# Converting weights inside the mixing of a spectral layer: the absolute value ahead of the relu, earlier matrices, one low part by DMA

## The chip, the cores and the metric

The kernel runs on one core of a Trainium2 chip. The metric is the time of one execution in device microseconds; a median of three executions is given, and one more execution was taken with the profiler. The engines are called PE (matmuls), DVE, ACT and POOL; SP only issues transfers, and POOL issues those transfers that add to what lies in the destination.

## The reference, cut to what matters

```python
X = np.fft.rfft(x, axis=1)                       # x: 2 x 3008 x 256
Yr = Xr @ w_r - Xi @ w_i + b_r                   # the mixing
Yi = Xr @ w_i + Xi @ w_r + b_i
Yr = np.sign(Yr) * np.maximum(np.abs(Yr) - 0.01, 0.0)
Yi = np.sign(Yi) * np.maximum(np.abs(Yi) - 0.01, 0.0)
y = np.fft.irfft(Yr + 1j * Yi, n=3008, axis=1)   # 6016 tokens of 256
h = y @ w_in1;  z = (h * sigmoid(1.702 * h)) @ w_out1     # 256 -> 2048 -> 256
h = z @ w_in2;  out = (h * sigmoid(h)) @ w_out2
```

The four matrices of the two MLP layers arrive as 64-bit floats. The kernel turns them into 32-bit floats itself, 128 x 512 numbers at a time. That work is called a conversion here, and the change is about where conversions stand.

## The kernel before, in words

There are four stages: the forward transform by matrices (until about 62 us), the mixing (62 to 147 us), the inverse transform by matrices (133 to 195 us, its PE part beginning while DVE still mixes), and the two MLP layers (the other 970 us). Up to the end of the inverse transform each engine's instructions stand in the order in which the Python code issues them. Nothing is reordered, so an instruction that waits holds up all that stands behind it on its engine.

**The mixing** is a loop of twelve turns, one for each unit (a batch, a parity, a block of 128 frequencies). In turn i the code issues, in this order:

- PE: the matmuls of unit i (`mid_mm`, L539 for units 0 and 1, L542 and L545 for the rest) into two PSUM banks. There are four banks for even and four for odd units, and the inverse transform uses the same eight.
- the sums of unit i-1 (`mid_sd`): ACT copies one bank (`us`, L551), DVE adds and subtracts (`sd`, L553 to L555). With L555 the banks are free again.
- the splits of the inputs of later units into a rounded high part and a low part (`xsplit`): ACT writes the negated value (L478), POOL adds the value by DMA (`xl`, L479), ACT casts the high part (L482).
- DVE: the folds of unit i-2 (`mid_fold`, `f`, L578; two more operations, L584 and L585, in some units).
- ACT: the relu of unit i-1 (`th`, L561), then `pump()`, then DVE's minimum (L566, `mid_th`).
- in turns 8, 10 and 11, SP: a pair of inverse matrices (`load_m`, `m<-in_mi`, L137). The fourth pair is loaded at step 0 of the inverse transform.
- at the end of turns 1, 3, 5, 7 and 9, a new conversion (`window`).

**A conversion** (`cv_bits`) begins with an absolute value on ACT (`cv_c<-raw`, L175). It reads `raw`, of which there is one buffer, and writes `cv_c`, of which there is one too. Then six closures are put on a list: five DVE operations (L180 to L184, "the bits") and one that issues POOL's adding DMA `cv_a<-cv_c` (L185) and SP's load of the next `raw` (L162, L163 or L166). `pump()` runs that list. So the next absolute value waits for two transfers: the load of `raw`, and the DMA that still reads `cv_c`.

**Placing**: a finished conversion is split into a rounded high part and a low part. `place_in` makes four sums on DVE (L213 to L216) and calls `split`. With `lo_eng="D"` ACT writes the negative (L105) and the high part (L107) and POOL adds the source by DMA (L106); with an engine given, ACT writes the high part (L109) and that engine subtracts (L110).

**The inverse transform** has sixteen steps of two banks. For each, DVE adds and subtracts (`rt`, `ac`, L406, L672 to L688), ACT copies one bank (`eo`, L668), and POOL adds results into `yt` by DMA (L722). Placings and two conversions stand among the steps.

Of the kernel before, what the change touches and what calls it, by code (L numbers as in the profile page):

```python
# [8 lines left out]

F32 = mybir.dt.float32  # L10
CFG = {'lv0': 'V', 'lv': 'V', 'dd0': 'VPVVPPPPPVVP', 'dd': 'V', 'ths': 'VVVVPV', 'thf': 'V', 'ivf': 'V', 'cva': 'P', 'pol': 'PPPP', 'pil': 'P', 'mvl': 'PVVP', 'xl': 'V', 'xse': 'V', 'gl': 'VPPPPPPP', 'tf': [6, 10, 13], 'tm': [1, 3, 5, 7, 9], 'ml': [], 'pk': 6, 'ti': [3, 7], 'pi': 4, 'pl': [1, 4, 8, 10, 13], 'kb': [0, 1, 1, 1, 1, 1, 1, 0], 'kr': [0, 1, 0, 1, 0, 1, 1, 0], 'fa': 3, 'xp': [2, 4, 4, 5], 'xq': [1, 4, 1], 'xs': 4, 'xi': [7, 7, 9, 10, 10, 11, 8], 'xsi': 9, 'xo': (0, 1, 6, 2, 3, 4, 5), 'xd': (0, 1, 4, 6), 'ca': 4, 'tl': True, 'fwd': 'all', 'rest0': 'all', 'rest1': 'all', 'last1': 'all', 'inv': 'all', 'mid': 'all', 'last0': 'all', 'thm': 'A', 'gl0': 'PVPVVVPV', 'gl2': 'PPPPPPPP', 'gl3': 'PPPPPPPV', 'xl0': 'VVVVVPV', 'xl1': 'V', 'pre': 13, 'pre2': 0, 'yd': 6, 'lvb': 6, 'mlp': 'all', 'pr': 'V', 'pf': 'V', 'eo': '0111', 'n32': 2, 'li': [8, 10, 11], 'lii': [0], 'xa': 4, 'nhb': 6, 'ddb': 6, 'mlp1': 'all', 'mlp2': 'all'}
NUM = dict(li=[5, 6, 7, 8], n32=2, pk=4, ydp=2, lii=[1, 3], xd=(), ml=[], pl=[], xo=range(7), pi=6, nhb=6, tf=[5, 9, 13], tm=[1, 3, 5, 7, 9, 11], ti=[0, 2, 4, 6, 8, 10, 12, 14, 14, 15, 15], kb=[2] * 8, kr=1, fa=3, fe=2, pm=0, nf=4, lvb=6, ddb=8, ivb=1, eob=1, fsb=6, f1=3, f2=0, fm=[7, 8, 9], fi=[1, 1, 2, 2], pre=13, pre2=1, yd=3, psh=0, ie=[12], xp=[1, 3, 4, 5], xq=[1, 2, 2], xs=5, nw=4, xi=[14, 14, 15, 15], xsi=13, rw=2, ca=4, cc=2, tb=1, tmn=1)

DEF = dict(pr="V", pf="V", lv0="V", lv="VPP", dd0="VVVVVP", dd="VPV", mpl="PV", ths="VP", thf="VVPP", fsl="VP", ivf="PPVV", cva="P", pol="P", pil="P", mvl="V", xl="PPVVPPP", xl0="PPVVPPP", xl1="PPVVPPP", xse="VP", gl="P", gl0="P", gl2="P", gl3="P", wcl="V", thc="V", thm="V")
# [42 lines left out]
def spectral_mlp_kernel(ctx, tc, xin, mfwd, minv, wc, bias, w_in1, w_out1, w_in2, w_out2, outT):  # L57
    nc = tc.nc
# [34 lines left out]
    cv_p = opened("cv", "left", 2)  # L93
# [56 lines left out]
    loaded, bits, added, fill = [], [], [], []  # L150
# [15 lines left out]
                nc.sync.dma_start(out=raw[:, :].rearrange("p (r d) -> p r d", r=2), in_=src)  # L166
            loaded.append(((kind, l, p, kept), raw))

    def cv_bits(raw, tag="a"):
        w = raw.bitcast(U32).rearrange("p (n t) -> p n t", t=2)  # L170
        hf = raw.bitcast(F32).rearrange("p (n t) -> p n t", t=2)[:, :, 1]
        c = cv_p.tile([P, 2 * CU], F32, tag="c", name="cv_c", bufs=1)
        a = cv_p.tile([P, 2 * CU], F32, tag=tag, name="cv_a", bufs=3 if tag == "a" else 1)
        cu, au = c.bitcast(U32), a.bitcast(U32)
        nc.scalar.activation(c, hf, AF.Abs, scale=2.0**-112)  # L175
        ts, stt = nc.vector.tensor_scalar, nc.vector.scalar_tensor_tensor
        band, bor, shl = ALU.bitwise_and, ALU.bitwise_or, ALU.logical_shift_left
# [57 lines left out]
    def settle(now=False):  # L235
        pump()
        ended[:] = []
        for u, (a, c) in bits:
            if not u[3]:
                spilled[u[:3]] = d = dram_p.tile([P, 2 * CU], F32, name=f"w_{u[0]}{u[1]}_{u[2]}")  # L240
                nc.sync.dma_start(out=d, in_=a)
        fresh = [(u, a) for u, (a, _) in bits if u[3]]
        done, added[:] = (added + fresh, ()) if now else (added[:], fresh)
        bits[:] = []
        return done

    def window(k, done, now=False, tag="a"):
        for u, a in done:
            if u[0] == "in":
                sums, puts = place_in(u[1], u[2], a, nc.vector if u[2] == NPR // 2 else "D", sums_tmp)  # L250
                if now:
                    for f in (puts[0], *sums, puts[1]):
                        f()
                else:
                    fill.extend(sums + puts)
            else:
                place_out(u[1], u[2], a, nc.gpsimd if u[2] == NPR - 2 else "D")
        for _ in range(min(k, len(loaded))):
            u, raw = loaded.pop(0)
            bits.append((u, cv_bits(raw, tag)))  # L260

    def tick(k=1):
        window(k, settle(True))
# [18 lines left out]
    raws, lvs, xs = {}, {}, {}  # L282
# [307 lines left out]
    hold = []  # L590
    for i in range(len(mids)):
        ps = mid_mm(i)
        sd = mid_sd(*post) if post is not None else None
        xsplit(i + 3, 1)
        xsplit(i + 2, 0)
        if thr is not None:
            mid_fold(*thr)
        if sd is not None:
            thr = mid_relu(*sd)
            pump()  # L600
            thr = mid_th(*thr)
# [323 lines left out]
    puts = []  # L925
# [11 lines left out]
    done = []  # L937
    added.extend(hold)
    for at, (l, i, p) in enumerate(seq):
# [8 lines left out]
        k = rate(at)  # L948
# [182 lines left out]
```

## Time and profile before

| | |
|---|---|
| median of three runs | 1166.54 us (1165.54 to 1167.99) |
| the profiled execution's own time | 1166.52 us |
| its span, first to last instruction | 1164.7 us |
| PE busy | 1146.9 us (98%) |
| DVE, ACT, POOL busy | 629.7, 774.4, 477.9 us |
| mean granted clock of PE | 0.995 |

The execution's time is 1.8 us more than its span. Over the whole span PE is idle for 17.8 us. What a change to the first 195 us can win is some of that idle time, and time in which PE runs at a lower clock. In the rows below, a time in square brackets is how long the engine sat idle before that instruction, and the arrow names what ended the wait.

### The profile page before, as it was taken

Reading aid. Unit: us, or ns where it says so; the run is one execution under the profiler, and the core shown is the slowest. Engines: PE = TensorE matmul, PEld = TensorE weight load, DVE = VectorE, ACT = ScalarE, POOL = GpSimd, SP = SyncE. Lnnn points to the kernel's source line nnn. Section 1 sums busy time; section 2 is a strip of 40 time slices with the busy share of each in tenths; the row PEclk is TensorE's granted clock in tenths of the full one; section 3 lists DMA queues with packets and bytes.
Section 4 is the critical chain, followed back from the end, with each engine's and each line's share of the span. In section 5 each row is a group of like instructions: output and inputs, shape, how many; then the busy total and the mean of one; then the engine's idle time right before and its main releaser. Section 6 shows DMA issues by size and latency. Waiting matters only on the chain.

```text
span 1164.7 us, 14637 instructions
## 1 busy us (share of the span) xinstructions
PE 1146.9 (98%) x5094; PEld 949.7 (82%) x5094; DVE 629.7 (54%) x1013; ACT 774.4 (66%) x1444; POOL 477.9 (41%) x412
## 2 busy tenths in 40 slices
PE   8999899999999999999999999999999999999998
PEld 6768786887888888888889878888888888888897
DVE  7777798766365474575563553442533523523522
ACT  2576446877677667676677786665766765766755
POOL 1243134454444443444436655333433333433333
PEclk9999899999999999999999999999999999999999
DMA  8777666451121121211220100000000000000000
GB/s 295 179 142 149 149 149 119 109 113 33 49 72 37 36 73 37 60 49 37 72 55 19 55 19 19 1 37 1 1 37 1 30 7 1 37 1 1 37 1 32
DMA packets 39564, 68.49 MB, mean 59 GB/s; under 512 B 3649, under 2 KB 15809, under 8 KB 39490
## 3 DMA queue, kind: packets, MB, share of 16 engines
q1 hardware_dynamic: 26162, 45.51, 11.9%
q0 software_dynamic: 13328, 22.05, 11.2%
q8 instruction: 40, 0.66, 0.2%
q14 instruction: 34, 0.28, 0.1%
HBM read 35.15 MB, written 10.35 MB: 39 GB/s over the span
## 4 chain that ended last, share of the span: by engine, by line
PE 81%; issue 7%; ACT 3%; DVE 3%; DMA 3%; POOL 2%; SPq 0%; POOLq 0%; DVEq 0%; ACTq 0%
PE o L808 40%; PE x L836 35%; PE psf L376 4%; PE psm L539 1%; ACT yt L839 1%; DMA cv_a<-cv_c 1%; DMA wo<-cv_a 1%; POOL xl L479 1%; ACT g L841 1%; DMA raw<-in_x 1%; DVE yt L858 0%; DMA xl<-xt 0%; POOL yt L722 0%; ACT x L747 0%; DVE yt L887 0%
## 5 line engine op out<-in xcount | busy, mean ns | idle before, releaser
L846 POOL TENSOR_TENSOR g<-yt,g 128x512 fp32r<-128x512 f32 (+1 forms) x282 | 362.7, 1298 | 495.8 <-PE x L836 332.0
L808 PE MATMUL o<-g,wo 128*128 128x512 f32 (+1 forms) x2304 | 560.1, 385 | 0.5 <-DMA wo<-cv_a 0.5
L836 PE MATMUL x<-x,wi 128*128 128x512 f32 (+1 forms) x2016 | 498.8, 386 | 3.5 <-ACT yt L877 1.9
L808 PEld LDWEIGHTS o<-g,wo 128*128 128x128 f32 x2304 | 432.4, 188 | 81.5 <-DMA wo<-cv_a 1.0
L836 PEld LDWEIGHTS x<-x,wi 128*128 128x128 f32 x2016 | 377.0, 188 | 80.4 <-ACT yt L877 4.9
L839 ACT ACTIVATE yt<-yt 128x512 f32<-128x512 f32 (+1 forms) x288 | 179.1, 622 | 253.6 <-DVE yt L887 204.8
L841 ACT CAST g<-yt 128x512 fp32r<-128x512 f32 (+1 forms) x384 | 235.1, 612 | 12.2
L887 DVE TENSOR_TENSOR yt<-yt,x 128x512 f32<-128x512 f32 (+1 forms) x96 | 64.7, 674 | 214.3 <-PE x L836 213.7
L858 DVE TENSOR_TENSOR yt<-yt,x 128x512 f32<-128x512 f32 (+1 forms) x96 | 64.8, 675 | 167.1 <-ACT yt L855 165.2
L846 DVE TENSOR_TENSOR g<-yt,g 128x512 fp32r<-128x512 f32 (+1 forms) x102 | 70.1, 687 | 73.2 <-ACT g L841 73.2
L185 POOL DMA_DIRECT2D cv_a<-cv_c x32 | 28.1, 877 | 98.4 <-DVE cv_c L184 92.0
L891 DVE TENSOR_TENSOR yt<-yt,x 128x512 f32<-128x512 f32 (+1 forms) x96 | 64.8, 674 | 0.4 <-issue 0.3
L754 DVE TENSOR_TENSOR x<-yt,x 128x512 fp32r<-128x512 f32 (+1 forms) x44 | 46.2, 1051 | 29.6 <-ACT x L747 29.6
L875 ACT COPY yt<-x 128x512 f32<-128x512 f32 (+1 forms) x96 | 54.7, 570 | 2.9 <-PE x L836 2.9
L839 ACT ACTIVATE yt<-x 128x512 f32<-128x512 f32 (+1 forms) x96 | 56.1, 584 | 0.0
L877 ACT COPY yt<-x 128x512 f32<-128x512 f32 (+1 forms) x96 | 55.7, 580 | 0.1
L376 PE MATMUL psf<-m,xf 128*128 128x190 f32 (+3 forms) x224 | 53.2, 399 | 2.4 <-POOL xf L327 2.4
L376 PE MATMUL psi<-m,f 128*128 128x188 f32 (+3 forms) x224 | 49.0, 373 | 6.2 <-DVE sd L555 2.9
L855 ACT COPY yt<-x 128x512 f32<-128x512 f32 (+1 forms) x96 | 54.7, 570 | 0.0
L376 PEld LDWEIGHTS psf<-m,xf 128*128 128x128 f32 x224 | 39.3, 193 | 16.1 <-POOL xf L327 3.0
L376 PEld LDWEIGHTS psi<-m,f 128*128 128x128 f32 x224 | 39.7, 199 | 13.8 <-DVE sd L555 3.2
L175 ACT ACTIVATE cv_c<-raw 128x512 f32<-128x512 f32 x32 | 21.5, 673 | 19.0 <-DMA cv_a<-cv_c 8.7
(118 smaller groups left out, 817.5 us busy)
## 6 DMA issues: line engine op xcount, KB each, us to landing
raw<-in_wi SPq DMA_DIRECT2D x32, 256.0 KB, 3.7
cv_a<-cv_c POOLq DMA_DIRECT2D x32, 256.0 KB, 5.1
raw<-in_wo SPq DMA_DIRECT2D x16, 512.0 KB, 3.9
xl<-xt POOLq DMA_DIRECT2D x20, 256.0 KB, 4.3
out_t<-yt SPq DMA_DIRECT2D x20, 256.0 KB, 2.0
raw<-in_x SPq DMA_DIRECT2D x9, 512.0 KB, 6.0
w_in<-cv_a SPq DMA_DIRECT2D x8, 256.0 KB, 2.0
w_out<-cv_a SPq DMA_DIRECT2D x8, 256.0 KB, 2.0
```

What stands on the lines that cost most here:

```text
L376: nc.tensor.matmul(ps, hi[:, c : c + P], m[:, k, :w], start=i == 0, stop=i == last)
L808: nc.tensor.matmul(acc[h, mm], st, mv, start=first and k == 0, stop=last and k == 2)
L836: nc.tensor.matmul(ps, st, mv, start=first and m == 0, stop=m == 2, skip_group_check=True)
L839: nc.scalar.activation(g, g if src is None else src, func)
L841: nc.scalar.copy(gh, g)
L846: eng.tensor_sub(gl, g, r32(gh))
L855: nc.scalar.copy(y1, X)
L858: nc.vector.tensor_add(y1, y1, Y)
L875: nc.scalar.copy(y2, Z)
L877: nc.scalar.copy(y3, X)
L887: nc.vector.tensor_add(y2, y2, X)
L891: nc.vector.tensor_add(y3, y3, Z)
```

## The change

Four things change. In turns 1, 3, 5, 7 and 9 the block that starts a conversion stands ahead of the folds and the relu and no longer at the end of the turn; `pump()` still stands behind the relu, so the bits now follow in the same turn. The pairs of inverse matrices are loaded in turns 3, 5 and 7. The fifth w_in unit (p = 4) of the first layer gets its low part by DMA like the others. The buffer tag of the last conversion is now found from a number; the tags come out the same.

```diff
-'li': [8, 10, 11]        (in the long CFG line)
+'li': [3, 5, 7]
-                sums, puts = place_in(u[1], u[2], a, nc.vector if u[2] == NPR // 2 else "D", sums_tmp)
+                sums, puts = place_in(u[1], u[2], a, "D", sums_tmp)
...
         xsplit(i + 3, 1)
         xsplit(i + 2, 0)
+        if i in N('tm'):
+            ready = settle(True)
+            window(0, [r for r in ready if r[0][2] < NPR // 2 and r[0][0] == "in"])
+            hold.extend(r for r in ready if r[0][2] >= NPR // 2 or r[0][0] == "out")
+            window(1, (), n=N('tm').index(i))
         if thr is not None:
             mid_fold(*thr)
         if sd is not None:
             thr = mid_relu(*sd)
-            pump()
+        pump()
+        if sd is not None:
             thr = mid_th(*thr)
         if i in N('li'):
             load_m()
         post = (i, ps)
-        if i in N('tm'):
-            ready = settle(True)
-            window(0, [r for r in ready if r[0][2] < NPR // 2 and r[0][0] == "in"])
-            hold.extend(r for r in ready if r[0][2] >= NPR // 2 or r[0][0] == "out")
-            window(1, (), tag="ld" if i == N('tm')[-1] else "a")
```

ACT in turns 9 and 10, with the last conversion of the mixing (before with -, now with +; the numbers of raw only count buffers):

```order
 L482 CAST xh<-xt_318 128x512
 L482 CAST xh<-xt_319 128x512
+L175 ACTIVATE cv_c<-raw_1127 128x512
 L561 ACTIVATE th<-sd,neglam 128x512 x2
-L175 ACTIVATE cv_c<-raw_1173 128x512
 L551 COPY us<-psm 128x512
 L561 ACTIVATE th<-sd,neglam 128x512 x2
```

The absolute value has moved ahead of the two halves of the relu of unit 8; the same holds in turns 1, 3, 5 and 7.

DVE before, from the folds of unit 8 in turn 10 to the sums of unit 10 in turn 11:

```order
L578 TENSOR_TENSOR f_1262<-th 128x512
L578 TENSOR_TENSOR f_1264<-th 128x512
L180 TENSOR_SCALAR cv_c<-cv_c 128x512
L181 TENSOR_SCALAR cv_c<-cv_c 128x512
L182 SCALAR_TENSOR_TENSOR cv_a<-raw_1173,cv_c 128x512
L183 TENSOR_SCALAR cv_c<-cv_a 128x512
L184 SCALAR_TENSOR_TENSOR cv_c<-raw_1173,cv_c 128x512
L566 SCALAR_TENSOR_TENSOR th<-sd,th 128x512 x2
L553 TENSOR_TENSOR sd<-us,psm 128x512
L554 TENSOR_TENSOR sd<-us,psm 128x256
L555 TENSOR_TENSOR sd<-psm,us 128x256
```

DVE now, from the last conversion's bits in turn 9 to the minimum of unit 9 in turn 10, ahead of the sums of unit 10:

```order
L180 TENSOR_SCALAR cv_c<-cv_c 128x512
L181 TENSOR_SCALAR cv_c<-cv_c 128x512
L182 SCALAR_TENSOR_TENSOR cv_a<-raw_1127,cv_c 128x512
L183 TENSOR_SCALAR cv_c<-cv_a 128x512
L184 SCALAR_TENSOR_TENSOR cv_c<-raw_1127,cv_c 128x512
L566 SCALAR_TENSOR_TENSOR th<-sd,th 128x512 x2
L553 TENSOR_TENSOR sd<-us,psm 128x512
L554 TENSOR_TENSOR sd<-us,psm 128x256
L555 TENSOR_TENSOR sd<-psm,us 128x256
L578 TENSOR_TENSOR f_1276<-th 128x512
L578 TENSOR_TENSOR f_1278<-th 128x512
L566 SCALAR_TENSOR_TENSOR th<-sd,th 128x512 x2
```

The same five operations now stand one whole turn earlier: between them and the sums of unit 10 lie the sums of unit 9, the folds of unit 8 and two minimums, where one minimum lay before.

SP before, from the load of turn 5 on:

```order
L166 DMA raw_1058<-in_wo 128x2x256
L166 DMA raw_1173<-in_wo 128x2x256
L137 DMA m<-in_mi 128x768 x2
L166 DMA raw_1275<-in_wo 128x2x256
L137 DMA m<-in_mi 128x760 x2
L137 DMA m<-in_mi 128x752 x2
L137 DMA m<-in_mi 128x1128 x2
```

SP now, the same loads:

```order
L137 DMA m<-in_mi 128x768 x2
L166 DMA raw_1006<-in_wo 128x2x256
L137 DMA m<-in_mi 128x760 x2
L166 DMA raw_1127<-in_wo 128x2x256
L137 DMA m<-in_mi 128x752 x2
L166 DMA raw_1239<-in_wo 128x2x256
L137 DMA m<-in_mi 128x1128 x2
```

Three pairs now stand ahead of the raw loads of turns 5, 7 and 9, and the fourth, at step 0 of the inverse transform, directly behind the load of turn 9.

## Rows read from the trace of the kernel before

**Rows 1.** Waits of PE, 130 to 200 us: engine, line, what ended it

```profile
PE psi L376 <- DVE sd L555: 2.9, 1, 2.9
PE psi L376 <- DVE rt L406: 2.0, 2, 1.3
PE x L836 <- DVE yt L887: 0.8, 1, 0.8
PE psi L376 <- DVE rt L688: 0.8, 1, 0.8
PE psi L376 <- DMA m<-in_mi: 0.5, 1, 0.5
PE x L836 <- ACT eo L668: 0.2, 1, 0.2
```

**Rows 2.** Timeline of PE, mixing and start of the inverse: start, length, instruction

```profile
81.79 0.39 PE L542 MATMUL psm<-wh,xh 128*128 128x512 f32 x1
...
87.47 0.39 PE L542 MATMUL psm<-wh,xh 128*128 128x512 f32 x1
...
132.91 4.06 PE L376 MATMUL psi<-m,f 128*128 128x192 f32 x24
139.91 2.93 PE L376 MATMUL psi<-m,f 128*128 128x192 f32 x8 [2.94 <-DVE sd L555]
```

**Rows 3.** Stretches: length, busy PE PEld DVE ACT POOL, clock, DMA share, GB/s

```profile
140.00:146.00 6.00, 5.54 (x17) 5.04 (x18) 5.93 (x11) 2.84 (x5) 0.00 (x0) 0.50 1.00 298
147.00:160.00 13.00, 13.00 (x83) 13.00 (x82) 12.04 (x26) 4.01 (x7) 1.75 (x3) 1.00 0.19 76
160.00:190.00 30.00, 26.98 (x117) 19.65 (x116) 27.86 (x53) 18.88 (x35) 20.06 (x21) 1.00 1.11 193
```

**Rows 4.** Timeline of DVE, 132 to 156 us

```profile
132.13 0.69 DVE L553 TENSOR_TENSOR sd<-us,psm 128x512 f32<-128x512 f32 x1 [4.05 <-ACT us L551]
...
134.60 0.42 DVE L180 TENSOR_SCALAR cv_c<-cv_c 128x512 f32<-128x512 f32 x1
...
137.31 1.29 DVE L566 SCALAR_TENSOR_TENSOR th<-sd,th 128x512 f32<-128x512 f32 x2
138.51 0.68 DVE L553 TENSOR_TENSOR sd<-us,psm 128x512 f32<-128x512 f32 x1
...
142.18 0.68 DVE L553 TENSOR_TENSOR sd<-us,psm 128x512 f32<-128x512 f32 x1
...
148.63 0.55 DVE L676 TENSOR_TENSOR rt<-psi,eo 128x380 f32<-128x380 f32 x1
...
154.44 0.55 DVE L110 TENSOR_TENSOR wi<-cv_a,wi 128x384 fp32r<-128x384 f32 x1
...
155.51 0.54 DVE L687 TENSOR_TENSOR ac<-rt,psi 128x377 f32<-128x377 f32 x1
```

**Rows 5.** Timeline of ACT, 116 to 150 us

```profile
116.76 0.67 ACT L175 ACTIVATE cv_c<-raw 128x512 f32<-128x512 f32 x1 [2.58 <-DMA cv_a<-cv_c]
...
130.96 0.66 ACT L175 ACTIVATE cv_c<-raw 128x512 f32<-128x512 f32 x1 [4.52 <-DMA cv_a<-cv_c]
131.53 0.57 ACT L551 COPY us<-psm 128x512 f32<-128x512 f32 x1
...
149.87 0.48 ACT L668 COPY eo<-psi 128x384 f32<-128x384 f32 x1 [5.22 <-DVE rt L406]
```

**Rows 6.** Waits of DVE, 60 to 150 us

```profile
DVE sd L553 <- ACT us L551: 11.9, 4, 4.0
```

**Rows 7.** Timeline of POOL, end of the mixing

```profile
137.69 0.86 POOL L185 DMA_DIRECT2D cv_a<-cv_c  x1 [13.32 <-DVE cv_c L184]
```

**Rows 8.** DMA issues, 109 to 119 us: transfer, count, KB, median us to landing

```profile
cv_a<-cv_c POOLq DMA_DIRECT2D x1, 256.0 KB, 5.5
```

**Rows 9.** DMA issues, 121 to 133 us, two matrices and a raw load beside it

```profile
cv_a<-cv_c POOLq DMA_DIRECT2D x1, 256.0 KB, 7.4
```

**Rows 10.** The buffer cv_a, 60 to 210 us: landing, shortest, median, longest

```profile
DMA to landing us min/median/max: 3.2/5.6/10.0
```

More of the change, by code (lines that the diff above doesn't have):

```diff
@@ L10 @@
 F32 = mybir.dt.float32
-CFG = {'lv0': 'V', 'lv': 'V', 'dd0': 'VPVVPPPPPVVP', 'dd': 'V', 'ths': 'VVVVPV', 'thf': 'V', 'ivf': 'V', 'cva': 'P', 'pol': 'PPPP', 'pil': 'P', 'mvl': 'PVVP', 'xl': 'V', 'xse': 'V', 'gl': 'VPPPPPPP', 'tf': [6, 10, 13], 'tm': [1, 3, 5, 7, 9], 'ml': [], 'pk': 6, 'ti': [3, 7], 'pi': 4, 'pl': [1, 4, 8, 10, 13], 'kb': [0, 1, 1, 1, 1, 1, 1, 0], 'kr': [0, 1, 0, 1, 0, 1, 1, 0], 'fa': 3, 'xp': [2, 4, 4, 5], 'xq': [1, 4, 1], 'xs': 4, 'xi': [7, 7, 9, 10, 10, 11, 8], 'xsi': 9, 'xo': (0, 1, 6, 2, 3, 4, 5), 'xd': (0, 1, 4, 6), 'ca': 4, 'tl': True, 'fwd': 'all', 'rest0': 'all', 'rest1': 'all', 'last1': 'all', 'inv': 'all', 'mid': 'all', 'last0': 'all', 'thm': 'A', 'gl0': 'PVPVVVPV', 'gl2': 'PPPPPPPP', 'gl3': 'PPPPPPPV', 'xl0': 'VVVVVPV', 'xl1': 'V', 'pre': 13, 'pre2': 0, 'yd': 6, 'lvb': 6, 'mlp': 'all', 'pr': 'V', 'pf': 'V', 'eo': '0111', 'n32': 2, 'li': [8, 10, 11], 'lii': [0], 'xa': 4, 'nhb': 6, 'ddb': 6, 'mlp1': 'all', 'mlp2': 'all'}
+CFG = {'lv0': 'V', 'lv': 'V', 'dd0': 'VPVVPPPPPVVP', 'dd': 'V', 'ths': 'VVVVPV', 'thf': 'V', 'ivf': 'V', 'cva': 'P', 'pol': 'PPPP', 'pil': 'P', 'mvl': 'PVVP', 'xl': 'V', 'xse': 'V', 'gl': 'VPPPPPPP', 'tf': [6, 10, 13], 'tm': [1, 3, 5, 7, 9], 'ml': [], 'pk': 6, 'ti': [3, 7], 'pi': 4, 'pl': [1, 4, 8, 10, 13], 'kb': [0, 1, 1, 1, 1, 1, 1, 0], 'kr': [0, 1, 0, 1, 0, 1, 1, 0], 'fa': 3, 'xp': [2, 4, 4, 5], 'xq': [1, 4, 1], 'xs': 4, 'xi': [7, 7, 9, 10, 10, 11, 8], 'xsi': 9, 'xo': (0, 1, 6, 2, 3, 4, 5), 'xd': (0, 1, 4, 6), 'ca': 4, 'tl': True, 'fwd': 'all', 'rest0': 'all', 'rest1': 'all', 'last1': 'all', 'inv': 'all', 'mid': 'all', 'last0': 'all', 'thm': 'A', 'gl0': 'PVPVVVPV', 'gl2': 'PPPPPPPP', 'gl3': 'PPPPPPPV', 'xl0': 'VVVVVPV', 'xl1': 'V', 'pre': 13, 'pre2': 0, 'yd': 6, 'lvb': 6, 'mlp': 'all', 'pr': 'V', 'pf': 'V', 'eo': '0111', 'n32': 2, 'li': [3, 5, 7], 'lii': [0], 'xa': 4, 'nhb': 6, 'ddb': 6, 'mlp1': 'all', 'mlp2': 'all'}
 NUM = dict(li=[5, 6, 7, 8], n32=2, pk=4, ydp=2, lii=[1, 3], xd=(), ml=[], pl=[], xo=range(7), pi=6, nhb=6, tf=[5, 9, 13], tm=[1, 3, 5, 7, 9, 11], ti=[0, 2, 4, 6, 8, 10, 12, 14, 14, 15, 15], kb=[2] * 8, kr=1, fa=3, fe=2, pm=0, nf=4, lvb=6, ddb=8, ivb=1, eob=1, fsb=6, f1=3, f2=0, fm=[7, 8, 9], fi=[1, 1, 2, 2], pre=13, pre2=1, yd=3, psh=0, ie=[12], xp=[1, 3, 4, 5], xq=[1, 2, 2], xs=5, nw=4, xi=[14, 14, 15, 15], xsi=13, rw=2, ca=4, cc=2, tb=1, tmn=1)
@@ L167, in cv_load, with cv_bits @@
             loaded.append(((kind, l, p, kept), raw))
-    def cv_bits(raw, tag="a"):
+    def cv_bits(raw, n):
         w = raw.bitcast(U32).rearrange("p (n t) -> p n t", t=2)
@@ L172, in cv_bits @@
         c = cv_p.tile([P, 2 * CU], F32, tag="c", name="cv_c", bufs=1)
-        a = cv_p.tile([P, 2 * CU], F32, tag=tag, name="cv_a", bufs=3 if tag == "a" else 1)
+        a = cv_p.tile([P, 2 * CU], F32, tag="ld" if n == 4 else "a", name="cv_a", bufs=1 if n == 4 else 3)
         cu, au = c.bitcast(U32), a.bitcast(U32)
@@ L245, in settle, with window @@
         return done
-    def window(k, done, now=False, tag="a"):
+    def window(k, done, now=False, n=0):
         for u, a in done:
             if u[0] == "in":
-                sums, puts = place_in(u[1], u[2], a, nc.vector if u[2] == NPR // 2 else "D", sums_tmp)
+                sums, puts = place_in(u[1], u[2], a, "D", sums_tmp)
                 if now:
@@ L259, in window @@
             u, raw = loaded.pop(0)
-            bits.append((u, cv_bits(raw, tag)))
+            bits.append((u, cv_bits(raw, n)))
     def tick(k=1):
```

## The prediction

> **What bounds the kernel now.** I read the waits of PE first, since PE is busy for 98% of the span and only its gaps can be won. Between 130 and 200 us they come to 7.2 us: 2.9 us at DVE's L555, 0.5 us at an inverse matrix, and 2.0, 0.8, 0.8 and 0.2 us at operations of the inverse transform's end work [rows 1]. Next I read PE's timeline for the place of the long one. It lies inside the second step of the inverse transform: 24 matmuls run from 132.91, then PE stands for 2.94 us until 139.91 [rows 2]. The stretches then show what followed: from 140 to 146 us the granted clock is 0.50, which is 1.2 GHz, the lower of the two levels, and from 147 us on it is 1.00 again [rows 3].
>
> Then I followed the wait back. PE needs banks that DVE frees with the sums of unit 10. These begin at 138.51, though the matmuls of unit 10 were over when those of unit 11 began, 5.68 us (one unit of 25 matmuls, as from 81.79 to 87.47) before 132.91 [rows 2, 4], at about 127. DVE is some 11 us behind PE. It got there by four waits for ACT's copy, 11.9 us in all [rows 6]. The last of them, 4.05 us, ends at 132.13 [rows 4], and ACT's copy began only at 131.53, directly behind an absolute value that had itself waited 4.52 us for the DMA of the conversion before [rows 5]. So the path of the mixing is no engine's work; it is a ring: absolute value, bits, POOL's adding DMA, its landing, next absolute value. In turns 7 to 9 it took 130.96 - 116.76 = 14.2 us for two units [rows 5], and PE needs 2 x 5.68 = 11.4.
>
> **The change, part by part.**
>
> *The ring.* Before, the absolute value stood at the end of a turn and its bits came after the next unit's copy, sums and folds. Now they follow at once. What is left of the ring is ACT's 0.6 us [rows 5], from the first bit operation to the issue of the DMA 137.69 - 134.60 = 3.1 us [rows 4, 7], and the landing L: 3.7 + L. It keeps up with PE as long as L is under 11.4 - 3.7 = 7.7 us. The trace has 5.5 us for a conversion's DMA with no matrices beside it [rows 8] and 7.4 us for one with a pair of matrices and a raw load beside it [rows 9]; the longest of the whole stretch is 10.0 [rows 10]. Now each conversion of turns 3, 5 and 7 has a pair beside it, so I take the 7.4, from the same company, and keep 5.5 and 10.0 as bounds.
>
> *What queues behind the absolute value.* Where it must wait, the relu of the unit before, the next copy and the splits wait behind it on ACT, and on DVE the bits, then the minimum, then the next unit's sums. That is the same company as before, but one turn earlier against PE. DVE's own work fits: from 132.13 to 138.51 lie the sums, folds, bits and minimum of one turn, 6.4 us; the bits are 2.7 of it (134.60 to 137.31) [rows 4], so a turn without them is 3.7, and two turns take 2 x 3.7 + 2.7 = 10.1 of PE's 11.4 us. The work now moved into turn 1 is hidden by DVE's wait for PE there; without that cover it would put DVE back by the 2.7 us once, which the 1.3 us of slack in each pair of turns gives back.
>
> *The end of the mixing.* With no lag left, the sums of unit 11 begin when its matmuls end, at 132.9 instead of 142.18. Up to the first end work of the inverse transform DVE then needs what it needed before, 148.63 - 142.18 = 6.45 us [rows 4], so that work begins at 139.35 and not at 148.63: 9.3 us earlier. PE's 2.94 us go, because unit 10 is freed within 2 us of the 127 at which its matmuls end. So does the stretch at the lower clock, as its cause is gone: 5.54 us of PE work at half speed [rows 3], 2.8 us lost.
>
> *The matrices.* They now land some 30 us ahead of their use, so the 0.5 us goes [rows 1]. It would not go by the ring alone: the loads stood behind a raw load that waits for the bits. What they cost is their share of the DMA engines in turns 3 to 7, and that is in L. SP passes three pairs ahead of raw loads; each pair has two turns until the next raw load, so the queue is not what makes those wait.
>
> The Trainium skill, in "DMA: Bandwidth & Descriptors" (section "Issuing engines are not separate DMA queues"), says that transfers issued by SP and by POOL run on the same 16 DMA engines and interleave. The step from 5.5 to 7.4 us agrees [rows 8, 9]. This is the rule that speaks against the change: SP's matrices lengthen the landing that the ring consists of, and the second case below hangs on it.
>
> *The low part by DMA.* DVE loses two subtractions, 154.44 to 155.51, 1.1 us [rows 4], in a stretch in which it is busy for 12.04 of 13 us [rows 3]. ACT gets two more operations and POOL two more issues in the same place. ACT stood idle for 5.22 us just before [rows 5], and POOL was busy for 1.75 of the 13 us [rows 3]; the weights are first read in the MLP. I cost it at nothing. Without that cover it is about 1 us on ACT, and not below nothing.
>
> *The inverse transform.* DVE is busy for 27.86 of 30 us there and PE waits for it in four groups, 2.0 + 0.8 + 0.8 + 0.2 = 3.8 us [rows 1, 3]. DVE comes 9.3 + 1.1 = 10.4 us earlier. PE without any of its waits comes 2.9 + 0.5 + 2.8 + 3.8 = 10.0 us earlier. The smaller of the two decides, 10.0, with the two so close that what is late next is DVE again: any new wait of DVE beyond 0.4 us costs PE the same. For such waits (the bounds are 0, and 1.5 us if several come) I take 0.7. From 195 us on PE is the bound and nothing there is changed, so what is won stays.
>
> The sum: 10.0 - 0.7 = 9.3 us. The profiled execution took 1166.52 us, the median of the runs is 1166.54, so no correction is needed: 1157.2 us.
>
> **The rivals.**
>
> *The landing grows to about 10 us.* For it: the longest in the trace, the DMA share of 1.11 at 160 to 190 us [rows 3, 10], and turn 3 has a placing's two DMAs beside its pair. Against it: 7.4 in the nearest case [rows 9]. By the durations above the first relevant DMA is issued in turn 3 at about 88.4 us (unit 2 over at 81.79 [rows 2]; DVE's sums and folds, 3.7 - 1.2 = 2.5 us without the minimum; a placing's four sums, an estimated 1 us; then the 3.1). The absolute value of turn 9 then stands at 88.4 + L + 2 x (3.7 + L) = 95.8 + 3L, and the end work of the inverse begins 0.6 + 2.7 + 1.2 (the minimum, 137.31 to 138.51 [rows 4]) + 2 x 3.7 + 6.45 = 18.3 us later, at 114.1 + 3L. With L = 10 that is 144.1, which is 4.5 us earlier than before; with 1.1 for the subtractions DVE wins 5.6: 1160.9 us. From L = 8.4 on this case takes over from the forecast.
>
> *The same formula, on the other side.* For L = 11.9 DVE wins nothing (114.1 + 35.7 = 149.8 against 148.63 + 1.1); above that the change is slower, as the ring now holds the relu back three times while the matrices pass. At L = 13 it begins at 153.1, DVE is 3.4 us late and PE's hole is that much longer: 1166.5 + 3.4 = 1169.9 us. Against it: no landing over 10.0 in the trace.
>
> *The inverse stage is paced by its DMAs.* At 160 to 190 us the DMA share is 1.11 [rows 3], and these adding transfers, not DVE, may set when its buffers come free. Then the waits of 3.8 us stay and the new ones come near their size: 10.0 - 3.8 - 3.0 = 3.2 us won, 1163.3. Against it: nearly all waits of PE there name DVE or ACT [rows 1].
>
> *It does not do what it says:* the landing of raw, not of `cv_a`, ends the wait anew, and the ring is as long as before: 1166.5.
>
> **How the numbers follow.** The forecast (landing up to 8.4 us) has a chance of 0.66, and by itself a range of 1155.8 to 1159.0. The landing near 10 has 0.15, the DMA-paced inverse stage 0.08, no effect 0.05, the slower case 0.06. A measurement of this kernel can tell 0.2%, 2.3 us, from no change. Faster by that: 0.66 + 0.15 + 0.07 = 0.88; within it 0.06; slower 0.06. For 8 in 10 the range takes the forecast's own, half a microsecond of scatter below it, and the case of 10 us above it with a little of what lies beyond: 1155.3 to 1162.0.
>
> **What would show it.** Right: PE's timeline has no gap of more than 1 us between 127 and 150 us, and the granted clock is 1.00 there; DVE's waits for ACT's copy in the mixing fall from 11.9 us to under 3; ACT's absolute values in the mixing wait for under 2 us in all; the end work of the inverse begins at 139 to 140 us; DVE runs no L110 there; the last wait of PE before the MLP ends near 185 us and not at 195. Wrong: absolute values of turns 5, 7 and 9 that wait for `cv_a` by 2 us or more, each longer than the one before (landing near 10); PE waits in the inverse stage that stay at 3.8 us or grow, and name DMAs (paced by DMAs); a stretch at the lower clock anywhere from 100 to 190 us.

## The result and the profile after

The changed kernel takes 1155.70 us (median of four runs, 1155.53 to 1157.88) against 1167.26 us for the kernel before beside it (four runs, 1165.54 to 1168.42): a ratio of 0.9906 [0.9888, 0.9925], some 11 us faster. The profiled execution took 1155.86 us with a span of 1154.1, which is 10.6 us shorter than the span before. The forecast was 1157.2, within 1155.3 to 1162.0, so the measured time lies near the lower end of the range.

The waits of PE after, 130 to 200 us, stand against the six of [rows 1]:

```profile
PE x L837 <- DVE yt L888: 0.9, 1, 0.9
PE psi L376 <- DVE rt L689: 0.6, 1, 0.6
PE x L837 <- ACT eo L669: 0.2, 1, 0.2
```

The wait for L555, the matrix and the two waits for L406 are gone. What stays is the end of the inverse transform, where PE has nothing else left to run. PE's timeline after has no stop where [rows 2] have one of 2.94 us:

```profile
131.31 6.01 PE L376 MATMUL psi<-m,f 128*128 128x192 f32 x36
...
138.43 0.48 PE L376 MATMUL psi<-m,fd 128*128 128x188 f32 x2
...
151.00 18.89 PE L376 MATMUL psi<-m,f 128*128 128x190 f32 x94
170.46 4.06 PE L376 MATMUL psi<-m,f 128*128 128x376 f32 x12 [0.57 <-DVE rt L689]
...
184.05 2.35 PE L837 MATMUL x<-x,wi 128*128 128x512 f32 x9 [0.85 <-DVE yt L888]
```

The stretches after (columns as in [rows 3]) have the clock at 1.00, the upper level, where it was 0.50 from 140 to 146 us:

```profile
130.00:140.00 10.00, 10.00 (x61) 9.77 (x60) 7.67 (x14) 2.60 (x5) 0.00 (x0) 1.00 0.01 2
140.00:150.00 10.00, 10.00 (x64) 10.00 (x63) 9.66 (x21) 4.21 (x8) 5.13 (x5) 1.00 0.46 75
```

ACT's absolute values and POOL's adding DMAs after answer to [rows 5, 7]; this is the ring itself:

```profile
81.95 0.66 ACT L175 ACTIVATE cv_c<-raw 128x512 f32<-128x512 f32 x1
94.55 0.66 ACT L175 ACTIVATE cv_c<-raw 128x512 f32<-128x512 f32 x1 [1.14 <-DMA raw<-in_wi]
106.08 0.68 ACT L175 ACTIVATE cv_c<-raw 128x512 f32<-128x512 f32 x1 [1.31 <-DMA cv_a<-cv_c]
117.70 0.67 ACT L175 ACTIVATE cv_c<-raw 128x512 f32<-128x512 f32 x1 [2.84 <-DMA cv_a<-cv_c]
```

```profile
86.95 0.86 POOL L185 DMA_DIRECT2D cv_a<-cv_c  x1 [0.61 <-DVE cv_c L184]
98.34 0.86 POOL L185 DMA_DIRECT2D cv_a<-cv_c  x1 [4.81 <-DVE cv_c L184]
109.89 0.86 POOL L185 DMA_DIRECT2D cv_a<-cv_c  x1 [5.00 <-DVE cv_c L184]
```

From 94.55 to 98.34 is 3.8 us of work (3.7 was forecast), and from that issue to the next absolute value 7.7 us; the next turn has 3.8 and 7.8. A turn of the ring, from one absolute value to the next, is 11.5 and 11.6 us where the one in [rows 5] took 14.2. The absolute values of turns 7 and 9 still wait for `cv_a`, the second longer than the first; that of turn 5 waits for the load of `raw`. But at the end of the mixing DVE is not late any more, as its timeline against [rows 4] shows:

```profile
131.58 0.69 DVE L553 TENSOR_TENSOR sd<-us,psm 128x512 f32<-128x512 f32 x1 [1.83 <-PE psm L542]
...
138.03 0.55 DVE L677 TENSOR_TENSOR rt<-psi,eo 128x380 f32<-128x380 f32 x1
...
154.10 0.55 DVE L688 TENSOR_TENSOR ac<-rt,psi 128x377 f32<-128x377 f32 x1 [0.31 <-DMA yt<-ac]
```

The sums of unit 11 now wait for PE. They began at 142.18 and begin at 131.58, and the end work of the inverse follows after the same 6.45 us, at 138.03. L110 does not run there any more. No wait of DVE from 60 to 150 us names ACT's copy any more, where [rows 6] have 11.9 us. Two waits of the bits for their absolute value are there:

```profile
DVE cv_c L180 <- ACT cv_c L175: 2.2, 2, 1.3
```

One more wait names the absolute value, the one of 3.49 us ahead of the first sums. The name misleads: the sums do not read `cv_c`, and the kernel before waits as long at the same place, for PE's matmuls of unit 0. So it is no waiting for ACT. Before, then after:

```profile
69.24 0.69 DVE L553 TENSOR_TENSOR sd<-us,psm 128x512 f32<-128x512 f32 x1 [3.48 <-PE psm L539]
```

```profile
67.64 0.69 DVE L553 TENSOR_TENSOR sd<-us,psm 128x512 f32<-128x512 f32 x1 [3.49 <-ACT cv_c L175]
```

**How much of the 10.6 us is the change.** Not all. The mixing's matmuls ended at 132.91 and now end at 131.31, and the first conversions already stand 1.6 us earlier. The difference arises in the first 62 us, where the change moves nothing: in the execution before, the granted clock was lower from 10 to 15 us. One row of each, before and then after, with the columns of [rows 3]:

```profile
10.00:15.00 5.00, 5.00 (x11) 2.50 (x11) 4.09 (x8) 0.68 (x4) 1.91 (x6) 0.70 1.06 408
```

```profile
10.00:15.00 5.00, 4.55 (x14) 2.77 (x15) 3.67 (x8) 1.20 (x6) 1.08 (x5) 1.00 1.03 394
```

This differs from one execution to the next and not with the order: of the experiments below, the third has the old order and a clock of 1.00 there (mixing over at 131.27), the fourth the new order and 0.66 (132.97). Against an execution with the same clock at the start the spans differ by 1163.5 - 1154.1 = 9.4 us (third against after, which differ in the order and the matrices alone) and 1164.7 - 1156.4 = 8.3 us (before against fourth, without the low part). From the first matmul of the inverse to PE's last wait before the MLP it is 195.25 - 132.91 = 62.34 us before and 184.05 - 131.31 = 52.74 after: 9.6 us won in the stage that the change acts on. Of the 10.6 us, 1.6 are the start, 9.6 this stage, and about 0.6 are given back in the MLP; 0.4 of these are PE's waits there, which grew from 2.7 to 3.1 us.

### The profile page after: what moved, and what is told of

Read it like the earlier page. It is cut to its first block, busy times and chain, and to the rows that moved or that the text cites. A ratio compares the mean times of both kernels' runs of the same rounds, so it can differ in the third digit from the quotient of the medians.

```text
span 1154.1 us, 14647 instructions
## 1 busy us (share of the span) xinstructions
PE 1141.7 (99%) x5094; PEld 946.7 (82%) x5094; DVE 628.4 (54%) x1011; ACT 775.9 (67%) x1446; POOL 478.4 (41%) x414
## 3 DMA queue, kind: packets, MB, share of 16 engines
q0 software_dynamic: 13616, 22.51, 11.5%
## 4 chain that ended last, share of the span: by engine, by line
PE 92%; ACT 2%; DVE 2%; issue 2%; DMA 1%; POOL 1%; SPq 0%; POOLq 0%; DVEq 0%
PE o L809 42%; PE x L837 37%; PE psm L542 5%; PE psf L376 4%; PE psi L376 3%; PE psm L539 1%; ACT yt L840 1%; DMA raw<-in_x 1%; ACT x L748 0%; DVE yt L859 0%; DMA yt<-ac 0%; ACT yt L856 0%; DMA wo<-cv_a 0%; DVE x L755 0%; ACT g L842 0%
## 5 line engine op out<-in xcount | busy, mean ns | idle before, releaser
L376 PE MATMUL psi<-m,f 128*128 128x188 f32 (+3 forms) x224 | 45.3, 358 | 0.6 <-DVE rt L689 0.6
L748 ACT CAST x<-tmp 128x512 fp32r<-128x512 f32 (+1 forms) x36 | 22.1, 613 | 17.6 <-DVE tmp L757 15.7
```

The lines of the kernel that those rows point to most:

```text
L376: nc.tensor.matmul(ps, hi[:, c : c + P], m[:, k, :w], start=i == 0, stop=i == last)
```

## The experiments

The theory was the ring: the mixing is paced by absolute value, bits, DMA and landing, and the new order shortens it. The rivals were that the matrices or the low part bring the gain, and that the ring's landing L grows until it costs what the order wins. Each kernel was compared with the kernel before on the same chip.

**1. Only the order.** The block ahead of the folds and the bits in the same turn; `li` stays [8, 10, 11], and the low part stays on DVE.

> Only the new place of the conversions in the mixing; matrices in turns 8, 10 and 11 and the subtracting low part as before. Ring theory (the late conversions made DVE late, and that made PE's gap and the lower clock): the 2.94 us gap and the stretch at 1.2 GHz go, absolute values of turns 5, 7, 9 wait under 1 us in all since no matrices run beside the first two, DVE reaches the end work of the inverse at about 138 to 139 us; but the matrices of turns 10 and 11 stand behind turn 9's raw load only, so they still come early enough (issue near 122 to 129, landing 5 to 9 us); DVE keeps the 1.1 us of subtractions, so PE's waits in the inverse grow by about 1: 8 to 9 us faster than before, 1158. Rival (the early matrices carry the gain): the gap stays at 2 to 3 us and the time is within 2 us of before.

Measured: 1156.79 us, ratio 0.9921 [0.9906, 0.9935]. The order alone brings 9.5 us against 1166.29 for the kernel before. Its absolute values hardly wait:

```profile
104.72 0.67 ACT L175 ACTIVATE cv_c<-raw 128x512 f32<-128x512 f32 x1
115.12 0.67 ACT L175 ACTIVATE cv_c<-raw 128x512 f32<-128x512 f32 x1 [0.22 <-DMA cv_a<-cv_c]
```

The landings of turns 5 and 7 are 4.9 and 5.4 us there and the ring 10.3 to 10.4 us, yet the end work begins at 138.07, as in the changed kernel: PE is the bound. The wait of 0.5 us for a matrix went too, against my claim that it needs the earlier loads. I expected PE's waits in the inverse stage to grow by about 1 us against the changed kernel; they are 1.9 us against 1.6.

**2. Only the matrices, at turns 3, 5 and 7 in the old order.**

```
-'li': [8, 10, 11]
+'li': [3, 5, 7]
```

> Only the earlier matrices (turns 3, 5, 7). Ring theory: the gap at the second step of the inverse and the lower clock stay, since the ring is as long as before; the 0.5 us at a matrix goes; the conversions' DMAs of turns 4, 6 and 8 now run beside matrices and land in 7 to 8 us in place of 5.3 and 5.5, so DVE is later by 2 to 4 us at the sums of unit 10 and the gap grows to 4 to 7 us: 1 to 5 us slower than before. Rival (the early matrices carry the gain): 5 us faster or more.

Measured: 1166.59 us, ratio 0.9995 [0.9982, 1.0008]: no difference, where I expected a loss. I had counted the pairs that are added beside conversions but not the pair of turn 8 that leaves. The absolute value of turn 9, which waited 4.52 us in [rows 5], waits 1.95; that of turn 7 waits 4.16 us and not 2.58. PE's stop is shorter and the waits in the inverse are longer:

```profile
PE psi L376 <- DVE rt L406: 3.4, 3, 2.1
PE psi L376 <- DVE sd L555: 2.3, 1, 2.3
```

**3. Only the low part by DMA.**

```
-place_in(u[1], u[2], a, nc.vector if u[2] == NPR // 2 else "D", sums_tmp)
+place_in(u[1], u[2], a, "D", sums_tmp)
```

> Only the low part by DMA. DVE is the bound of the inverse stage: its end comes 1.1 us earlier, the gap and the lower clock stay: PE's waits there fall from 3.8 to about 2.7, 0.5 to 1.1 us faster, which is too small for the times to tell but is seen in the trace. Rival (what stands on DVE in the inverse stage is what counts most): 3 us or more.

Measured: 1166.42 us, ratio 0.9998 [0.9989, 1.0006]. Alone, the low part brings nothing that can be measured: PE still stops for 3.33 us at L555 and waits 2.5 us for L406. I expected its waits in the inverse stage to fall from 3.8 to about 2.7 us; they are 4.4. The lower clock behind the stop lasts about half as long here as before: 0.57 from 138 to 142 us and 1.00 from 142 to 146, where the kernel before has 0.66 and 0.50.

**4. Order and matrices, without the low part.**

> The whole change but for the low part, which DVE subtracts as before. Ring theory: like the changed kernel up to the first step of the inverse (no gap, clock 1.00, end work from about 138 us), then PE's waits in the inverse stage larger by about 1.1 us (2.7 in place of 1.6): 1156.5 to 1157. Rival (the subtraction on DVE decides): 1159 or more.

Measured: 1157.3 us, ratio 0.9917 [0.9903, 0.9932], the same as the order alone. The matrices lengthen the ring (absolute values wait 1.42 and 2.54 us for `cv_a`, landings of turns 5 and 7 of 7.9 and 7.4 us), but the PE waits from 130 to 200 us are those of the first experiment, 0.8, 0.8 and 0.2. A pair issued beside the transfer is not all there is to it: in the first experiment the matrices of turn 8 are issued 0.2 and 1.8 us behind the transfer of turn 7, and it still lands in 5.4 us.

What the low part does is seen at two places. The wait for L689 is 0.82 us here and in the first experiment, 0.57 in the changed kernel. And the 94 matmuls ahead of it take 18.89 us in the changed kernel, but 19.24 us here and 19.23 in the first experiment:

```profile
151.04 19.23 PE L376 MATMUL psi<-m,f 128*128 128x190 f32 x94
```

From the first matmul of the inverse to PE's last wait before the MLP it is 53.3 us in both, against 52.74. So the low part is worth 0.6 us on PE, where I expected 1.1 us of waits, and the order 9.0 of the 9.6 us.

**5. The changed kernel with the bits in the next turn again.** The absolute value stays ahead of the relu.

```
-        pump()
+        if i not in N('tm'):
+            pump()
```

> The changed kernel, but the bits of turns 1, 3, 5, 7 and 9 run in the next turn, as before the change; only the absolute value stays ahead of the relu. Ring theory: the ring is then longer than before the change, not shorter: absolute value, two relus, minimum, the next unit's sums and folds, bits, DMA, landing, that is about 0.6 + 1.3 + 1.2 + 1.3 + 1.2 (or 2.7) + 3.1 + 6 to 8 = 15 to 18 us for two turns against 11.4 that PE needs. The gap is back with 3 to 8 us, the clock falls again: 1166 to 1171, no gain or slower. Rival (it is the absolute value's place ahead of the relu that brings the gain): 1155 to 1158, no gap.

Measured: 1172.17 us, ratio 1.0043 [1.0028, 1.0058]: slower than before, and just above the 1166 to 1171 that I expected. The place of the absolute value is worth nothing without the bits behind it. The ring is longer than ever, and what it holds back on ACT now stops PE inside the mixing. ACT, then PE:

```profile
106.09 0.66 ACT L175 ACTIVATE cv_c<-raw 128x512 f32<-128x512 f32 x1 [6.68 <-DMA raw<-in_wi]
122.95 0.66 ACT L175 ACTIVATE cv_c<-raw 128x512 f32<-128x512 f32 x1 [8.64 <-DMA cv_a<-cv_c]
```

```profile
126.91 0.50 PE L542 MATMUL psm<-wh,xh 128*128 128x512 f32 x1 [4.53 <-ACT xh L482]
```

The turn of the ring is 122.95 - 106.09 = 16.9 us. The split `xh` of the next unit stands behind the absolute value on ACT, and PE waits for it. The other half, the bits in the same turn with the absolute value at its old place, was not run; so it is shown that the bits must follow, and not that the absolute value had to move.

**6. The kernel before with a second buffer for `cv_c`.** Conversions of turns 5 and 9 use another buffer, so from turn 5 on no absolute value waits for the landing before it; order, matrices and low part are as before.

```
-c = cv_p.tile([P, 2 * CU], F32, tag="c", name="cv_c", bufs=1)
+c = cv_p.tile([P, 2 * CU], F32, tag="tmp" if alt else "c", name="cv_c", bufs=1)
```

> The kernel before; only the conversions of turns 5 and 9 write their absolute value into another buffer (the one for sums, idle there), so that no absolute value from turn 5 on waits for the DMA that reads the buffer of the one before. Order, matrices and low part as before. Ring theory: the waits for cv_a, 2.6 and 4.5 us in turns 7 and 9, go; the ring then runs through the load of raw, 5.1 + 2.7 + 0.3 + 4.5 = 12.6 us for two turns in place of 13.7 to 14.2, so DVE is 3 to 5 us less late at the sums of unit 10: the gap shrinks to 1 us or less or goes, the clock may stay at 1.00: 3 to 6 us faster than before. Rival (DVE is late by its own work, not by the ring): gap and time as before.

Measured: 1162.98 us, ratio 0.9955 [0.9937, 0.9972]: 4.1 us faster. The ring is real, since opening it at another link helps too. The absolute values of turns 7 and 9, which waited 2.58 and 4.52 us for `cv_a`, now wait for `raw`, whose load is issued behind the bits:

```profile
117.46 0.68 ACT L175 ACTIVATE cv_c<-raw 128x512 f32<-128x512 f32 x1 [0.77 <-DMA raw<-in_wo]
128.24 0.67 ACT L175 ACTIVATE cv_c<-raw 128x512 f32<-128x512 f32 x1 [1.10 <-DMA raw<-in_wo]
```

So there are two rings, one through `cv_c` and one through `raw`, and both hold the bits. The second was there already in the kernel before; its absolute values of turns 3 and 5 wait for `raw`, the later one longer:

```profile
103.07 0.66 ACT L175 ACTIVATE cv_c<-raw 128x512 f32<-128x512 f32 x1 [4.30 <-DMA raw<-in_wi]
```

Moving the bits forward shortens both, which a buffer does not. PE's stops at 137 and 141 us are 0.67 and 1.88 us here, and the granted clock stays at 1.00 behind them.

**7. More bytes.** The changed kernel, with half again as many bytes beside each of the three pairs of matrices on SP's queue, into columns that nothing reads.

```
+            if nb * w < 1000:
+                o = cs * MW // 2 + nb * w
+                nc.sync.dma_start(out=m[:, o : o + 384], in_=minv[t // 2, q, cs][:, :384])
```

> The changed kernel, with half as many bytes again beside each of the three pairs of matrices, loaded into columns that nothing reads. Landing theory (the conversions' DMA shares the engines with them, and the mixing is late by three times what it grows): landings of the conversions' DMAs rise from 7.7 to about 9 us, the absolute values of turns 5, 7 and 9 wait for 2.5, 3.5 and 6 us in place of 1.1, 1.3 and 2.8; DVE's sums of unit 11 begin about 1 to 2 us after PE's matmuls end; 0 to 2 us slower than the changed kernel. Rival (the queue of SP does not touch POOL's DMAs): landings and waits as in the changed kernel.

Measured: 1155.85 us, ratio 0.9904 [0.9889, 0.9919]. I expected the landing to grow and it did not. The issues from 97 to 108 us, in the changed kernel and here:

```profile
xl<-xt POOLq DMA_DIRECT2D x4, 256.0 KB, 8.2
m<-in_mi SPq DMA_DIRECT2D x2, 380.0 KB, 8.0
...
cv_a<-cv_c POOLq DMA_DIRECT2D x1, 256.0 KB, 7.7
```

```profile
xl<-xt POOLq DMA_DIRECT2D x4, 256.0 KB, 9.2
m<-in_mi SPq DMA_DIRECT2D x2, 380.0 KB, 9.0
...
m<-in_mi SPq DMA_DIRECT2D x2, 192.0 KB, 10.1
cv_a<-cv_c POOLq DMA_DIRECT2D x1, 256.0 KB, 7.4
```

The matrices take a microsecond longer; `cv_a` does not. The time is what the rival gives, but its reason (SP's queue does not touch POOL's transfers) does not hold: the splits `xl`, which POOL issues behind `cv_a`, take a microsecond longer too. In the changed kernel SP's last matrix of this stretch lands at 107.05 us and `cv_a`, issued at 98.34, at 106.06. So SP's queue is busy for that whole landing already, and bytes behind it come too late to matter; the later `xl` outlast it, the last of them until 111.50, and meet the added bytes. That is how I read the rows; it was not tested further. The landing of turn 9, which gets no added bytes of its own, takes 8.5 us and not 7.9.

The Trainium skill, "DMA: Bandwidth & Descriptors" (section "Queues, rings and completion order"), says that a DMA engine takes a packet from each queue in turn. These rows agree with it (7.4 us for `cv_a` and 9.2 for `xl`); what each engine did packet by packet was not looked at.

**8. Is DVE the pace of the inverse stage?** The changed kernel with the final subtractions of the inverse transform on POOL; the final additions stay on DVE.

```
-'ivf': 'V'
+'ivf': 'VVVP'
```

> A try for a faster version: the changed kernel with one of the two kinds of final subtractions in the inverse transform (about 0.9 us each for three batches) on POOL and not on DVE. If DVE is still what PE waits for there, PE's 1.6 us of waits between 165 and 185 us go: about 1 to 1.5 us faster than the changed kernel, 1154.5. Rival (POOL's operation takes over 1.1 us and holds DVE at the shared buffers, or delays POOL's DMAs): as the changed kernel or 1 us slower.

Measured: 1161.4 us, ratio 0.9949 [0.9933, 0.9966], 5.6 us above the seventh kernel, which ran beside it. The rival was right, and by more than I put. POOL, DVE and PE of this kernel:

```profile
146.69 2.85 POOL L719 TENSOR_TENSOR yt<-rt 128x376 f32<-128x376 f32 x2 [2.42 <-DVE rt L689]
```

```profile
158.75 0.55 DVE L688 TENSOR_TENSOR ac<-rt,psi 128x377 f32<-128x377 f32 x1 [3.91 <-DMA yt<-ac]
```

```profile
159.99 11.76 PE L376 MATMUL psi<-m,f 128*128 128x376 f32 x48 [2.18 <-issue]
```

POOL's 2.85 us stand ahead of its adding DMAs, which were issued at 146.59 in the changed kernel and now at 149.50; 0.6 us of that is a later start of the inverse transform. DVE must have `ac` back from them, and waits 3.91 us where it waited 0.31. So the rival that the inverse stage is paced by its DMAs lies near: in the changed kernel DVE waits for them for only 0.31 us, and issued later they hold it for 3.91.

**9 and 10. A longer landing on POOL's own queue.** The changed kernel, with one or three copies of 256 KB to spare memory issued ahead of the adding DMA in turns 3, 5 and 7.

```
+    def copies(c):
+        for _ in range(1):          # 3 in the tenth
+            d = dram_p.tile([P, 2 * CU], F32, name=f"spare{len(spares)}")
+            spares.append(d)
+            nc.gpsimd.dma_start(out=d, in_=c)
-lambda: (nc.gpsimd.dma_start(out=a, in_=c, accum_op=ALU.add), ...
+lambda: (copies(c) if n in (1, 2, 3) else None, nc.gpsimd.dma_start(out=a, in_=c, accum_op=ALU.add), ...
```

> The changed kernel; in turns 3, 5 and 7 POOL copies the conversion's buffer to a spare place in HBM (256 KB) ahead of the conversion's adding DMA, so that this DMA lands later without a byte more on SP's queue. Landing theory, with the formula of the prediction moved by the 1.3 us by which the changed kernel's profiled execution was ahead when the mixing began: the absolute value of turn 9 at 94.5 + 3L, the end work of the inverse at 112.8 + 3L, but not before 138.0, where L is the time from the end of the bits to the landing. With L near 10: absolute value near 124, end work near 142.8, PE waits 3 to 5 us longer in the inverse stage: 1158 to 1161. Rival (DVE's slack takes it up): 1155 to 1157.

> The same with three such copies. With L near 13.5: absolute value of turn 9 near 135, end work near 153, PE's gap at the second step of the inverse is back with 7 to 10 us and the clock falls; 1167 to 1174, slower than the kernel before the change: the case on the other side of the prediction. If the gap is back and the time still under 1163, the formula takes the landing for too much.

Measured: 1156.75 us, ratio 0.9908 [0.9889, 0.9927], with one copy; 1163.44 us, ratio 0.997 [0.9957, 0.9983], with three. Both are quicker than expected, as the copies lengthened the landing by less than I put. With one copy the time is that of the rival: DVE's slack takes it up. With three the gap at the second step, which I expected back, is not there; PE waits later, in the inverse stage. With the landing that was measured the formula of the prediction holds for the places in the trace. It had the absolute value of turn 9 at 95.8 + 3L and the end work at 114.1 + 3L, that is 18.3 us later, and the forecast giving way from L = 8.4. Its 95.8 rested on a first issue estimated at 88.4; in the changed kernel this is the one at 86.95, 1.45 us earlier, so 94.35 + 3L, and L = (117.70 - 94.35) / 3 = 7.8 us. This L is a mean over turns 3, 5 and 7, up to what ended the wait: `cv_a` in turns 5 and 7, but in turn 3 the load of `raw`, at 94.44 us, as `cv_a` had landed there within 5.6. With one copy (its line is 8 higher), ACT and then DVE:

```profile
119.64 0.66 ACT L183 ACTIVATE cv_c<-raw 128x512 f32<-128x512 f32 x1 [4.14 <-DMA cv_a<-cv_c]
```

```profile
131.60 0.68 DVE L561 TENSOR_TENSOR sd<-us,psm 128x512 f32<-128x512 f32 x1
138.05 0.55 DVE L685 TENSOR_TENSOR rt<-psi,eo 128x380 f32<-128x380 f32 x1
```

Its first issue lies at 86.93, so L is (119.64 - 94.33) / 3 = 8.4 us. The absolute value waits 4.14 us, and the sums of unit 11 stand exactly where they stood in the changed kernel, with no wait for PE left: this is the point of change that was forecast. With three copies, ACT, DVE and PE:

```profile
126.97 0.66 ACT L183 ACTIVATE cv_c<-raw 128x512 f32<-128x512 f32 x1 [5.67 <-DMA cv_a<-cv_c]
```

```profile
145.37 0.55 DVE L685 TENSOR_TENSOR rt<-psi,eo 128x380 f32<-128x380 f32 x1
```

```profile
177.42 5.75 PE L384 MATMUL psi<-m,f 128*128 128x376 f32 x12 [0.82 <-DVE rt L697]
```

This execution had the lower clock at the start (0.66 from 10 to 15 us), with its first issue at 88.51, so L is (126.97 - 95.9) / 3 = 10.4 us. The end work begins 18.4 us behind the absolute value (18.3 forecast), and PE waits for DVE four times, 1.28, 1.50, 0.82 and 0.82 us. The case of a landing near 10 gives 1162.1 us for this L: the end work at 114.1 + 31.2 = 145.3 is 3.3 us earlier than before, with 1.1 for the subtractions 4.4 of 1166.5. Measured are 1163.44, and 1164.83 for the profiled execution, from which L is read; that is 2.7 us more. Of these 1.7 are the clock, which fell in this profile and not in that case: the last row's 12 matmuls take 5.75 us, and 4.06 in the changed kernel. Another 0.3 us is a wait of PE inside the mixing for `xl`, which stands behind the copies on POOL's queue; the rest was not followed. From 178 to 180 us:

```profile
178.00:180.00 2.00, 2.00 (x5) 1.04 (x4) 1.93 (x5) 0.58 (x2) 0.81 (x2) 0.50 1.11 260
```

The slower side of this rival (L above 11.9) was not reached.

## Why the prediction was right

The mechanism held, and so did its size in the stage that the change acts on: 9.6 us against 9.3. That two of the sum's terms erred against each other, and that the changed kernel's profiled execution was ahead from the start, was luck. These are its steps.

- *The ring decides the mixing.* Shown from three sides: shortening it alone brings 9.5 us (first), lengthening it to 16.9 us costs 5.1 against the kernel before (fifth; there ACT's splits stop PE as well), and opening it at another link brings 4.1 (sixth). But the prediction named one ring where there are two: in turns 3 and 5 the load of `raw` ended the wait before, and after it still does in turn 5, the mechanism of the rival to which I gave 0.05. It cost 1.14 us of waiting there and did no harm, since this load too is issued behind the bits.
- *3.7 + L.* 3.8 us, and 7.7, 7.8 and 7.9 us for the landings of turns 5, 7 and 9, against 7.4. In turn 3 it was 5.6, though a pair of matrices was loaded a microsecond later. The bound of 10.0 us was misread: [rows 10] hold every transfer that reads or writes `cv_a`, and the 10.0 is a placing (`wo<-cv_a`, issued at 173.90); the longest landing of a conversion from 60 to 210 us is 7.8. So "the longest in the trace" said nothing for the case of 10 us. The 11.5 us of a turn are just over PE's 11.4, so the absolute values wait a little more each time, 5.3 us in all. I had set under 2 as the mark, and that mark was wrong; the wait of 2.84 us in turn 9 even has the size that I had set as a sign of the case of 10 us. The mark for DVE, under 3 us for ACT's copy, held: none is left. There is cover for the ring: in the last turn DVE still waits 1.83 us for PE, and only at L = 8.4 is that used up (ninth).
- *The end work at 139.35.* At 138.03, and 139.69 in the fourth experiment, whose clock at the start was as low as in the kernel before.
- *The gap and the clock.* Both went, together, in every kernel with the new order and a landing up to 8.4 us. The clock cost a little more than the 2.8 us of the sum. PE's timeline before, further on from [rows 2]:

```profile
143.30 1.64 PE L376 MATMUL psi<-m,f 128*128 128x190 f32 x4 [0.46 <-DMA m<-in_mi]
...
146.70 0.48 PE L376 MATMUL psi<-m,fd 128*128 128x188 f32 x2
...
159.26 2.40 PE L376 MATMUL psi<-m,f 128*128 128x190 f32 x14
162.93 15.65 PE L376 MATMUL psi<-m,f 128*128 128x188 f32 x72 [1.27 <-DVE rt L406]
179.32 1.54 PE L376 MATMUL psi<-m,f 128*128 128x188 f32 x8 [0.74 <-DVE rt L406]
...
195.25 2.34 PE L836 MATMUL x<-x,wi 128*128 128x512 f32 x9 [0.85 <-DVE yt L887]
```

From the 25th matmul of the step at 139.91 to the second pair on `fd` at 146.70 PE worked for 6.8 - 0.46 = 6.3 us. After, the 25th of the 36 begins at 131.31 + 24 x 0.162 = 135.2, and that pair at 138.43: 3.2 us. So the lower clock cost 3.1 us in this execution. By the same count it is 1.7 us in the third experiment, where the stop is longer and the lower clock lasts half as long; the size of this term is that of one execution.
- *The waits of the inverse stage.* This term was mis-sized. The sum had 3.8 us of waits gone and 0.7 of new ones. Of the 3.8 only 2.2 went: 0.85 and 0.19 are the same after, and 0.57 of 0.82. These stand at the end of the stage, where PE has nothing else left to run. That was made good by what the wait column does not show: 94 matmuls in one piece take 18.89 us after, and the same in three pieces took 2.40 + 15.65 + 1.54 = 19.59 before, 0.7 us beside the waits. Not all of that comes with the two stops in brackets, as the first and fourth experiments have none there and take 19.23 and 19.24. Waits 7.2 - 1.6 = 5.6, clock 3.1 and these 0.7 make 9.4 of the measured 9.6 us.
- *The matrix wait.* "It would not go by the ring alone" is the step that failed. In the first experiment the pairs are still loaded in turns 8, 10 and 11, and no matrix is waited for. The raw load that they stand behind waits for the bits, and the bits come earlier: I had the right chain and did not follow it through. The matrices bring nothing that can be measured, with the new order (first against fourth) or the old (second).
- *The low part.* Costed at 1.1 us on DVE and nothing elsewhere; it is 0.6 us on PE with the new order, and alone nothing that can be measured.

The profiled execution was to take 1157.2 us and took 1155.86. That it is lower is the start, which no step of the prediction foresaw: with the 1.6 us put back, it is 1157.5.

## What to carry to other kernels

Where one engine's wait stands in a loop that leads through a buffer and a DMA, write the loop down with its times and set it against the time that the bounding engine needs for the same units: it tells both what a shorter link wins and from which landing time it wins no more. Operations on a buffer that others wait for belong directly behind the one that fills it, not a turn later; starting the first earlier and leaving the rest was worse than nothing here. An engine that only issues DMAs is not idle: work put ahead of an issue delays all that waits for the transfer.

## What the runs showed of the hardware

- A conversion's landing on POOL's queue of 4.9 us (first, turn 5) became 7.9 with 0.75 MB of matrices issued beside it by SP (fourth), and with half as much again it was 7.4 (seventh), while other transfers of POOL, `xl`, went from 8.2 to 9.2 us. It was 5.4 us in the first experiment and 5.6 in the changed kernel where the second matrix was issued more than 1.5 us behind it. Copies on POOL's own queue lengthened the way from the end of the bits to the next absolute value: 7.8 us without, 8.4 with one of 256 KB, 10.4 with three.
- Stops of PE of 2.27 us (second), 2.94 (before), 3.33 (third) and 4.53 (fifth) go with a stretch at a granted clock of 0.50, the lower level, that begins about where they end. Stops of 0.67 and 1.88 us (sixth), 2.08 (second and sixth), 1.91 and 2.16 (fifth) and 2.18 (eighth) do not. But in the tenth the clock fell to 0.50 behind waits of 0.82 and 0.82 us, and in the second once more at 180.5 us, behind 1.06 and 0.82. So the length of one stop doesn't tell it.
- The clock in the first 15 us differs between executions though no kernel changes that stretch: 0.66 to 0.72 from 10 to 15 us (before, fourth, fifth, sixth, tenth), or 1.00. Where it is low and nothing else stops PE, the mixing ends at 132.5 to 133.0 us; where it is 1.00, at 131.3, or at 131.9 in the second and eighth. Why is open.
